# Attention and feed-forward fused on one core: both query blocks of a head pair transposed in one go, and ScalarE's queue in the order of the program

## The chip, the cores and the metric

The kernel runs on one core of one Trainium2 chip. The metric is the device time of one execution in microseconds, as the median over the runs; lower is better. The kernel before takes 610.69 us (median of 3 runs, 610.4 to 610.88).

## What is computed

Attention over 4 batches, 8 heads, 768 positions and head size 64, in which a query sees the 8 first positions and the 96 last ones up to itself, with a distance bias per head; its output, 3072 tokens of 512 features, goes through a gated feed-forward without an activation function.

```python
scores = scale * np.matmul(q, k.transpose(0, 1, 3, 2)) + bias
scores = np.where(keep, scores, -1000000000.0)
a = np.exp(scores - np.max(scores, axis=-1, keepdims=True))
a = a / (np.sum(a, axis=-1, keepdims=True) + 1e-09)
x = np.matmul(a, v)            # then heads side by side: 3072 x 512
out = (((x @ w1) * (x @ w2)) @ w3) @ w_out
```

All matmuls are float32 in precision: operands are split into a high and a low half in the matmul's own format, and three products are summed (high-high, low-high, high-low). The product w3 @ w_out is formed once, at the start.

## The kernel before, in words

**Chunks and visits.** A chunk is 256 tokens of one batch; there are 12. A head pair of a chunk is 128 rows of queries in two blocks of 128 (j = 0, 1). Two head pairs make a visit, so a chunk takes two visits and the loop has 24 of them (s = 0 to 23), and a last one (s = 24) with the values alone. A visit s does this:

- TensorE multiplies the transposed probabilities of visit s - 1 with the values (`values`, L457 and L459) into one PSUM bank, pool `ps_v`, tag "v"; then the scores of visit s (L406).
- ScalarE and VectorE split that result into a high and a low half, `xh` and `xl` (`split`, L63 and L64).
- VectorE takes the scores with the bias and their minimum (L421), ScalarE the exponentials and their sum (L422): eight of each, one for each head of each block.
- The scalings by 1/sum (`softmax`, L434): for each block the first head on ScalarE, the second on VectorE (L436). In the first four visits all eight are on ScalarE.
- Four turns (`flip`): two or four 128x128 transposes on TensorE (L445, L447) into one PSUM bank (`ps_t`, tag "t", one buffer), which ScalarE evicts to `ph` (L449). There is one for each head pair and query block. At the start of a sequence the first block has only half the keys, and two transposes.

**Feed-forward between them.** `FeedForward.run` is a generator over 512 tokens (two chunks; 256 for the first two runs). For each of 8 blocks f of the hidden width it multiplies with w1 (12 matmuls, tile `m`, n = 0), lets ScalarE evict that to `a` (L168), multiplies with w2 (n = 1), lets VectorE form the product `g` (L171) and ScalarE and VectorE split it (`gh`, `gl`). Then the output rows follow in four tiles of 24 matmuls (L178 to L180) that ScalarE evicts to `ot` (L184). All these results share two PSUM banks (pool `ps_m`, two buffers): the matmuls of the next f and n = 0 wait until `a` has been evicted, those of n = 1 until `g` has been formed. The generator yields at half and whole of each group of 12 matmuls; such a piece of six matmuls is a slice, and `slices(k)` puts the next k of them into the program. A run of 512 tokens has 48 slices, 12 a visit; the table `SLICES` says how many stand ahead of each turn and behind the last.

**What sets the order.** Each engine works through its queue in order. TensorE's order is that of the program text throughout (`manual_schedule`). In `first_steps` (visits 0 to 3, together with the loading and conversion of the weights and with w3 @ w_out, `fold`, L142) VectorE's and the DMA queue's are too. Elsewhere a scheduler orders the instructions by its own estimate; this holds for ScalarE everywhere. In the first steps VectorE also turns the weights' bits into the matmul format (L54, L56, L58), ScalarE takes their high halves (`w1h`, `w2h`, L122) and VectorE the low ones (L130); `fold_and_turn` puts the eight folds of one block between the turns.

## Time and profile before

| what | value |
|---|---|
| median of 3 runs | 610.69 us |
| the profiled execution | 609.55 us, of which the span of the instructions is 607.8 us |
| TensorE (PE) busy | 578.6 us, 95% of the span |
| ScalarE (ACT) busy | 287.6 us, 47% |
| VectorE (DVE) busy | 261.3 us, 43% |
| mean DMA rate | 89 GB/s |
| granted TensorE clock | 0.998 |

How to read it: PE is TensorE, PEld its weight loads, ACT ScalarE, DVE VectorE, SP the DMA queue's engine. In a row of the timeline stand the start in us from the start of the span, the duration, the engine, the line, the instruction, its tiles (out<-in), its shapes and how many were merged; in brackets the idle time of its engine just before it and who ended that. Matmuls overlap: each shows a duration that is longer than the step from one start to the next, so what TensorE loses is read from the starts.

### The profile page before, as it was taken

Reading aid. Unit: us, or ns where it says so; the run is one execution under the profiler, and the core shown is the slowest. Engines: PE = TensorE matmul, PEld = TensorE weight load, DVE = VectorE, ACT = ScalarE, POOL = GpSimd, SP = SyncE. Lnnn points to the kernel's source line nnn. Section 1 sums busy time; section 2 is a strip of 40 time slices with the busy share of each in tenths; the row PEclk is TensorE's granted clock in tenths of the full one; section 3 lists DMA queues with packets and bytes.
Section 4 is the critical chain, followed back from the end, with each engine's and each line's share of the span. In section 5 each row is a group of like instructions: output and inputs, shape, how many; then the busy total and the mean of one; then the engine's idle time right before and its main releaser. Section 6 shows DMA issues by size and latency. Waiting matters only on the chain.

```text
span 607.8 us, 9908 instructions
## 1 busy us (share of the span) xinstructions
PE 578.6 (95%) x3872; PEld 455.5 (75%) x3872; DVE 261.3 (43%) x851; ACT 287.6 (47%) x777; POOL 1.3 (0%) x10
## 2 busy tenths in 40 slices
PE   2998998999999999999999999999999999999995
PEld 0444568989977787887787887787878778888884
DVE  8999998432334424304442322542342451212200
ACT  3065677654455635525544544653553653522210
POOL 0000000000000000000000000000000000000000
PEclk9999999999999999999999999999999999999999
DMA  8897653222023202211220330120331120000001
GB/s 305 304 340 253 212 208 116 79 80 78 27 71 95 78 2 77 79 65 50 78 70 8 113 113 1 61 63 1 125 100 34 44 78 18 36 17 1 0 27 48
DMA packets 23240, 54.01 MB, mean 89 GB/s; under 512 B 2704, under 2 KB 4752, under 8 KB 23184
## 3 DMA queue, kind: packets, MB, share of 16 engines
q1 hardware_dynamic: 23184, 53.29, 25.7%
q8 instruction: 32, 0.52, 0.4%
q14 instruction: 24, 0.20, 0.1%
HBM read 46.99 MB, written 6.29 MB: 88 GB/s over the span
## 4 chain that ended last, share of the span: by engine, by line
PE 70%; ACT 13%; DVE 12%; issue 2%; DMA 2%; SPq 0%; DVEq 0%; ACTq 0%
PE m L161 11%; PE m L163 11%; PE m L162 10%; PE o L178 7%; PE o L180 7%; PE o L179 7%; ACT pr L422 7%; PE v L457 3%; PE t L445 3%; PE t L447 3%; ACT pr L434 3%; PE v L459 3%; PE w L142 2%; PE s L406 2%; DVE t L56 1%
## 5 line engine op out<-in xcount | busy, mean ns | idle before, releaser
L422 ACT ACTIVATE pr<-pr,mx 128x232 f32<-128x232 f32 (+1 forms) x192 | 88.4, 462 | 47.7 <-DVE mx L421 47.7
L449 ACT ACTIVATE ph<-t 128x512 f32<-128x512 f32 (+1 forms) x96 | 53.9, 561 | 101.5 <-PE t L447 93.1
L171 DVE TENSOR_TENSOR g<-m,a 128x512 f32<-128x512 f32 x48 | 33.2, 691 | 142.7 <-PE m L163 131.1
L161 PE MATMUL m<-xh,w1h 128*128 128x512 f32 (+1 forms) x224 | 85.8, 383 | 6.8 <-ACT a L168 6.8
L161 PE MATMUL m<-xh,w2h 128*128 128x512 f32 (+1 forms) x224 | 82.9, 370 | 0.3 <-ACT a L168 0.3
L163 PE MATMUL m<-xh,w1l 128*128 128x512 f32 (+1 forms) x224 | 80.8, 361 | 0.0
L162 PE MATMUL m<-xl,w1h 128*128 128x512 f32 (+1 forms) x224 | 80.7, 360 | 0.0
L163 PE MATMUL m<-xh,w2l 128*128 128x512 f32 (+1 forms) x224 | 80.7, 360 | 0.0
L162 PE MATMUL m<-xl,w2h 128*128 128x512 f32 (+1 forms) x224 | 80.5, 359 | 0.0
L178 PE MATMUL o<-wh,gh 128*128 128x512 f32 x192 | 78.2, 407 | 0.0
L180 PE MATMUL o<-wh,gl 128*128 128x512 f32 x192 | 75.3, 392 | 0.0
L179 PE MATMUL o<-wl,gh 128*128 128x512 f32 x192 | 75.0, 390 | 0.0
L142 PE MATMUL w<-wo,t 128*128 128x512 f32 x128 | 61.0, 622 | 12.1 <-DVE wo L58 11.2
L64 DVE TENSOR_TENSOR xl<-v,xh 128x512 fp32r<-128x512 f32 x24 | 16.6, 690 | 121.0 <-ACT xh L63 120.9
L63 ACT ACTIVATE gh<-g 128x512 fp32r<-128x512 f32 x48 | 30.2, 630 | 64.6 <-DVE g L171 64.6
L161 PEld LDWEIGHTS m<-xh,w1h 128*128 128x128 f32 x224 | 42.2, 189 | 20.0 <-ACT a L168 11.9
L142 PEld LDWEIGHTS w<-wo,t 128*128 128x128 f32 x128 | 24.1, 198 | 40.0 <-issue 22.4
L421 DVE CUSTOM_DVE_ANT_0 pr<-s,biasw 128x232 f32<-128x232 f32 x160 | 53.4, 394 | 0.0
L445 PE MATMUL t<-ident,pr 128*128 128x128 f32 x192 | 45.8, 273 | 3.7 <-ACT pr L434 3.4
L64 DVE TENSOR_TENSOR gl<-g,gh 128x512 fp32r<-128x512 f32 x48 | 33.2, 692 | 34.4 <-ACT gh L63 34.4
L161 PEld LDWEIGHTS m<-xh,w2h 128*128 128x128 f32 x224 | 42.3, 189 | 6.8 <-issue 0.7
L163 PEld LDWEIGHTS m<-xh,w1l 128*128 128x128 f32 x224 | 42.2, 189 | 6.7
(84 smaller groups left out, 816.1 us busy)
## 6 DMA issues: line engine op xcount, KB each, us to landing
qr<-qk SPq DMA_DIRECT2D x32, 312.0 KB, 3.8
vr<-vx SPq DMA_DIRECT2D x32, 256.0 KB, 3.0
stage<-w3t SPq DMA_DIRECT2D x15, 512.0 KB, 6.4
out_dram<-ot SPq DMA_DIRECT2D x24, 256.0 KB, 2.0
raws<-w SPq DMA_DIRECT2D x10, 512.0 KB, 5.7
qr<-qk SPq DMA_DIRECT2D x16, 260.0 KB, 3.4
vr<-vx SPq DMA_DIRECT2D x16, 192.0 KB, 2.7
stage<-w SPq DMA_DIRECT2D x6, 512.0 KB, 7.2
```

What stands on the lines that cost most here:

```text
L64: nc.vector.tensor_tensor(out=lo, in0=x, in1=hi.bitcast(F32), op=ALU.subtract)
L142: nc.tensor.matmul(ps, lhsT=self.t3[f, z][:, i * P:(i + 1) * P].bitcast(F32), rhs=self.wo[:, k].bitcast(F32), start=k == 0, stop=k == NFC - 1)
L161: nc.tensor.matmul(ps[:, z], lhsT=mh, rhs=xh[:, i], start=i == 0, stop=False)
L162: nc.tensor.matmul(ps[:, z], lhsT=mh, rhs=xl[:, i], start=False, stop=False)
L163: nc.tensor.matmul(ps[:, z], lhsT=ml, rhs=xh[:, i], start=False, stop=i == NCC - 1)
L178: nc.tensor.matmul(ps, lhsT=gh[:, f, ts], rhs=self.wh[:, f], start=f == 0, stop=False)
L179: nc.tensor.matmul(ps, lhsT=gh[:, f, ts], rhs=self.wl[:, f], start=False, stop=False)
L180: nc.tensor.matmul(ps, lhsT=gl[:, f, ts], rhs=self.wh[:, f], start=False, stop=f == NFC - 1)
L421: nc.vector.tensor_tensor_reduce(out=pr[:, j, u, w0:], in0=ps[u][:, j, w0:UW], in1=bias, scale=-SCALE, scalar=3.0e38, op0=ALU.add, op1=ALU ...
L422: nc.scalar.activation(pr[:, j, u, w0:], pr[:, j, u, w0:], AF.Exp, bias=m, scale=-1.0, accum_out=sm[:, j, u:u + 1])
L445: nc.tensor.transpose(pt[:, u, 0], pr[:, j, u, BW:UW], ident)
L449: nc.scalar.activation(ph[:, :, :nk], pt[:, :, :nk], AF.Copy)
```

## The change

The second query block of a head pair is transposed right behind the first, in the PSUM bank of the values, and `turn` does both. In the table each visit has two turns in place of four. In the loop from visit 4 on, ScalarE's order too is that of the program, and there the first two slices stand ahead of the scalings instead of behind them. In `fold_and_turn` the folds are divided 4, 3 and 1 around the two turns.

```diff
-        pt = ps_t.tile([P, 2, 2, P], F32, tag="t", name=f"t_{c}_{hp}_{j}")
+        pool, tag = ((ps_t, "t"), (ps_v, "v"))[j]
+        pt = pool.tile([P, 2, 2, P], F32, tag=tag, name=f"t_{c}_{hp}_{j}")
...
-    def turn(s, m, prs):
-        phs.setdefault(s, []).append(flip(*pairs(s)[m // NQ], m % NQ, prs[m // NQ][0]))
+    def turn(s, i, prs):
+        phs.setdefault(s, []).extend(flip(*pairs(s)[i], j, prs[i][0]) for j in range(NQ))
...
-            for m in range(STEP * NQ):
-                ff.fold(f, 2 * m, 2 * m + 1)
-                turn(s, m, prs)
+            ff.fold(f, 0, 1, 2, 3)
+            turn(s, 0, prs)
+            ff.fold(f, 4, 5, 6)
+            turn(s, 1, prs)
+            ff.fold(f, 7)
...
-        for m in range(STEP * NQ):
-            turn(3, m, prs)
-            slices(SLICES[3][m + 1])
+        for i in range(STEP):
+            turn(3, i, prs)
+            slices(SLICES[3][i + 1])
...
-    SLICES = [()] * 3 + [(4, 2, 2, 1, 1)] * 3 + [(4, 2, 1, 1, 1)] * 2 + [(5, 2, 2, 2, 1)] * (n - 8)
+    SLICES = [()] * 3 + [(4, 4, 2)] * 3 + [(4, 3, 2)] * 2 + [(5, 4, 3)] * (n - 8)
...
-        for s in range(4, n + 1):
-            rs = all_rows(s, visit(s))
-            for p, r in zip(pairs(s), rs):
-                softmax(*p, *r, nc.vector)
-            if s == n:
-                break
-            loads(s + 1)
-            for m in range(STEP * NQ):
-                slices(SLICES[s][m])
-                turn(s, m, rs)
-            slices(SLICES[s][-1])
-        slices(10 ** 6)
+        with tc.manual_schedule(engines={mybir.EngineType.Activation}):
+            for s in range(4, n + 1):
+                rs = all_rows(s, visit(s))
+                if s == n:
+                    break
+                slices(2)
+                for p, r in zip(pairs(s), rs):
+                    softmax(*p, *r, nc.vector)
+                loads(s + 1)
+                slices(SLICES[s][0] - 2)
+                for i in range(STEP):
+                    turn(s, i, rs)
+                    slices(SLICES[s][i + 1])
+            slices(10 ** 6)
```

Two places show what moves. The first is ScalarE's queue in a visit of the loop (visit 17, chunk 8; the lines of `flip` are two further down in the changed file). Before, from the exponentials (L422) on:

```order
L422 ACTIVATE pr_2_3641,sm_2_3643<-pr_2_3641,mx_2_3642 128x232 x4
L422 ACTIVATE pr_3_3652,sm_3_3654<-pr_3_3652,mx_3_3653 128x232 x4
L434 ACTIVATE pr_2_3641<-pr_2_3641,sm_2_3643 128x232 x2
L434 ACTIVATE pr_3_3652<-pr_3_3652,sm_3_3654 128x232 x2
L168 ACTIVATE a_3_3696<-m_3_0_3683 128x512
L63 ACTIVATE gh_3478<-g_3_3711 128x512
L449 ACTIVATE ph_2_0_3727<-t_2_0_3722 128x512
L168 ACTIVATE a_4_3735<-m_4_0_3715 128x512
L449 ACTIVATE ph_2_1_3749<-t_2_1_3744 128x512
L63 ACTIVATE gh_3478<-g_4_3757 128x512
```

and in the changed kernel:

```order
L422 ACTIVATE pr_2_3643,sm_2_3645<-pr_2_3643,mx_2_3644 128x232 x4
L422 ACTIVATE pr_3_3654,sm_3_3656<-pr_3_3654,mx_3_3655 128x232 x4
L168 ACTIVATE a_3_3678<-m_3_0_3665 128x512
L434 ACTIVATE pr_2_3643<-pr_2_3643,sm_2_3645 128x232 x2
L434 ACTIVATE pr_3_3654<-pr_3_3654,sm_3_3656 128x232 x2
L63 ACTIVATE gh_3460<-g_3_3713 128x512
L451 ACTIVATE ph_2_0_3729<-t_2_0_3724 128x512
L451 ACTIVATE ph_2_1_3736<-t_2_1_3731 128x512
L168 ACTIVATE a_4_3744<-m_4_0_3717 128x512
L63 ACTIVATE gh_3460<-g_4_3759 128x512
L451 ACTIVATE ph_3_0_3775<-t_3_0_3770 128x512
L451 ACTIVATE ph_3_1_3782<-t_3_1_3777 128x512
```

The eviction of the first feed-forward tile, `a_3`, has moved from behind the four scalings to ahead of them, and the evictions of a head pair's two blocks stand side by side. VectorE's and the DMA queue's orders are the same as before but for two swaps of neighbours on VectorE in visit 7.

The second place is TensorE's queue in the first steps, in `fold_and_turn(5, 1)` (`w_518` is the tile of the fold, `t_2` and `t_3` the two head pairs). Before:

```order
L142 MATMUL w_518<-wo,t_5_0_343 128x512 x2
L445 MATMUL t_2_0_521<-ident,pr_2_442 128x128 x2
L142 MATMUL w_518<-wo,t_5_0_343 128x512 x2
L445 MATMUL t_2_1_528<-ident,pr_2_442 128x128
L447 MATMUL t_2_1_528<-ident,pr_2_442 128x128
L445 MATMUL t_2_1_528<-ident,pr_2_442 128x128
L447 MATMUL t_2_1_528<-ident,pr_2_442 128x128
L142 MATMUL w_518<-wo,t_5_1_344 128x512 x2
L445 MATMUL t_3_0_537<-ident,pr_3_453 128x128 x2
L142 MATMUL w_518<-wo,t_5_1_344 128x512 x2
```

and in the changed kernel:

```order
L142 MATMUL w_518<-wo,t_5_0_343 128x512 x4
L447 MATMUL t_2_0_523<-ident,pr_2_442 128x128 x2
L447 MATMUL t_2_1_528<-ident,pr_2_442 128x128
L449 MATMUL t_2_1_528<-ident,pr_2_442 128x128
L447 MATMUL t_2_1_528<-ident,pr_2_442 128x128
L449 MATMUL t_2_1_528<-ident,pr_2_442 128x128
L142 MATMUL w_518<-wo,t_5_1_344 128x512 x3
L447 MATMUL t_3_0_538<-ident,pr_3_453 128x128 x2
```

Four folds stand ahead of the first turn instead of two, the second block follows the first without folds between, and one fold is left behind the last turn. ScalarE's queue, which the scheduler still orders here, has at this place:

```order
L451 ACTIVATE ph_2_0_526<-t_2_0_523 128x2x128
L451 ACTIVATE ph_2_1_533<-t_2_1_528 128x512
L451 ACTIVATE ph_3_0_541<-t_3_0_538 128x2x128
L451 ACTIVATE ph_3_1_548<-t_3_1_543 128x512
L144 ACTIVATE wh<-w_518 128x512
L122 ACTIVATE w1h<-t3s 128x512
L63 ACTIVATE xh_409<-v_2_565 128x2x256
L122 ACTIVATE w2h<-t3s 128x512
```

Before, `w1h` and `wh` stood between `ph_3_0` and `ph_3_1`, and `w2h` ahead of `xh`.

## The prediction

> **What bounds the kernel now.** I read the page first, then the list of waits, then the timeline of one visit of the loop and of the first steps. From the page come the span, TensorE's share and the clock:

> ```profile
> span 607.8 us, 9908 instructions
> ...
> PE 578.6 (95%) x3872; PEld 455.5 (75%) x3872; DVE 261.3 (43%) x851; ACT 287.6 (47%) x777; POOL 1.3 (0%) x10
> ...
> PEclk9999999999999999999999999999999999999999
> ```

> TensorE is busy for 95% of the span and the clock is full in all forty slices. An edit is worth what it takes from TensorE's waits, or adds. The list of waits (time in all, times, longest) names those that a turn or a scaling has part in:

> ```profile
> PE m L161 <- ACT a L168: 7.1, 13, 0.7
> ...
> PE t L445 <- ACT pr L434: 3.4, 2, 2.0
> ...
> DVE w2l L130 <- ACT w2h L122: 1.4, 3, 0.8
> ...
> DVE wl L147 <- ACT wh L144: 0.6, 1, 0.6
> ```

> The first is the largest: thirteen times the feed-forward's matmuls wait for a PSUM bank that `a` holds. The next rows are one such wait, from the timeline of visit 16, engine by engine (start, duration, engine, line, what; in brackets the idle time before and who ended it). TensorE, at the end of n = 1:

> ```profile
> 321.06 0.39 PE L162 MATMUL m<-xl,w2h 128*128 128x512 f32 x1
> 321.29 0.39 PE L163 MATMUL m<-xh,w2l 128*128 128x512 f32 x1
> 322.37 0.50 PE L161 MATMUL m<-xh,w1h 128*128 128x512 f32 x1 [0.69 <-ACT a L168]
> 322.71 0.39 PE L162 MATMUL m<-xl,w1h 128*128 128x512 f32 x1
> ```

> ScalarE and VectorE in the same stretch:

> ```profile
> 320.22 1.62 ACT L434 ACTIVATE pr<-pr,sm 128x232 f32<-128x232 f32 x4
> 321.74 0.57 ACT L168 ACTIVATE a<-m 128x512 f32<-128x512 f32 x1
> 323.07 0.63 ACT L63 ACTIVATE gh<-g 128x512 fp32r<-128x512 f32 x1 [0.76 <-DVE g L171]
> 324.51 0.60 ACT L449 ACTIVATE ph<-t 128x512 f32<-128x512 f32 x1 [0.80 <-PE t L447]
> ```

> ```profile
> 320.76 0.59 DVE L436 TENSOR_SCALAR pr<-pr,sm 128x232 f32<-128x232 f32 x2
> 322.35 0.69 DVE L171 TENSOR_TENSOR g<-m,a 128x512 f32<-128x512 f32 x1 [1.00 <-ACT a L168]
> ```

> The twelve matmuls of n = 1 take a step of 0.23 us each, so those of n = 0, which `a` evicts, were done about 12 steps before 321.29 + 0.39, at 318.9. ScalarE's exponentials end where its scalings begin, at 320.2; `a` stands behind the four scalings and starts only at 321.74. TensorE has then finished n = 1, and starts the next f at 322.37 instead of a step after 321.29.

> **The change part by part: `a` ahead of the scalings.** A matmul's step is 0.23 us (321.06 to 321.29). The wait makes it 1.08 us (321.29 to 322.37), 0.85 too long, and the next step is 0.34 instead of 0.23 (322.37 to 322.71), because the weight load starts late too: 0.96 us lost where the row reads 0.69 idle, so 0.27 more than the idle time each. Over the list: 7.1 us idle + 13 x 0.27 = 10.6 us. One of the thirteen lies in the first steps and is not of this kind:

> ```profile
> 100.79 0.39 PE L161 MATMUL m<-xh,w2h 128*128 128x256 f32 x1 [0.25 <-ACT a L168]
> ```

> It counts for 0.25 + 0.27 = 0.5 us; twelve waits in the loop remain, **10.1 us**. They are the three visits of each of four long runs that begin at n = 0 of some f.

> In the new order `a` stands right behind the exponentials. Its matmuls are done at 318.9, so it would start at 320.2 and end at 320.8; TensorE wants the bank at 321.5, a step after 321.29. The margin is 0.7 us and the whole wait goes. Where is the next one? `g` starts when the second group is done (321.29 + 0.39 = 321.7; VectorE's scalings end at 320.76 + 0.59 = 321.35) and ends at 322.4; its bank is wanted after twelve more matmuls and a turn of eight, at 321.5 + 2.7 + 0.9 = 325.1: margin 2.7 us. The scalings come 0.57 us later, 320.8 to 322.4, and a head pair needs half of them, by 321.6; the first turn stands behind one more slice, at 321.5 + 6 x 0.23 = 322.9: margin 1.3 us.

> **Two turns of eight for four of four.** The timeline of the same visit at its first turn:

> ```profile
> 323.87 0.27 PE L445 MATMUL t<-ident,pr 128*128 128x128 f32 x1
> 323.98 0.27 PE L447 MATMUL t<-ident,pr 128*128 128x128 f32 x1
> 324.09 0.27 PE L445 MATMUL t<-ident,pr 128*128 128x128 f32 x1
> 324.20 0.27 PE L447 MATMUL t<-ident,pr 128*128 128x128 f32 x1
> 324.23 0.48 PE L161 MATMUL m<-xh,w1h 128*128 128x512 f32 x1
> 324.55 0.39 PE L162 MATMUL m<-xl,w1h 128*128 128x512 f32 x1
> ```

> Four transposes with the matmul behind them take 323.87 to 324.55, 0.68 us, of which 0.23 is the matmul's: 0.45, or 0.11 each. There is no cost of going in and out, so eight in one go cost twice four: zero. Nor does ScalarE's count change.

> [...]

> **The bank of the values.** The second block needs that bank free. In each visit its last reader is VectorE's split, in this one:

> ```profile
> 315.38 0.69 DVE L64 TENSOR_TENSOR xl<-v,xh 128x512 fp32r<-128x512 f32 x1
> ```

> It ends at 316.1, 7 us ahead of the first turn. Between the turns lie four slices (24 x 0.23 = 5.5 us), behind the last three (4.1 us), and the two evictions take some 0.3 + 2 x 0.60 = 1.5 us after the last transpose (324.20 to 324.51, then the row's duration). The values queue behind this wait on TensorE, and everything behind them, but the margin is 2.6 us: zero.

> **The first steps.** TensorE's rows at visits 1 to 3, and ScalarE's scalings of visit 3:

> ```profile
> 59.56 0.62 PE L445 MATMUL t<-ident,pr 128*128 128x128 f32 x2 [2.05 <-ACT pr L434]
> ...
> 66.90 0.71 PE L457 MATMUL v<-ph,vr 128*64 128x128 f32 x8
> ...
> 96.41 0.33 PE L445 MATMUL t<-ident,pr 128*128 128x128 f32 x1 [1.38 <-ACT pr L434]
> ```

> ```profile
> 95.89 3.13 ACT L434 ACTIVATE pr<-pr,sm 128x232 f32<-128x232 f32 x8
> ```

> At 59.56 the first turn waits for the scalings; two more folds ahead of it fill most of that. A fold is 1.0 us at most: 7.34 us from 59.56 to 66.90, less twelve transposes at 0.11, by six folds. The values, at 66.90 now, would start up to 2 us earlier. But this is lent: at 96.41 the turn of visit 3 waits for scalings again, and those hang on VectorE's conversions, which run almost without a pause. So TensorE keeps only what VectorE gains: at most its waits for ScalarE in the list, 1.4 + 0.6 = 2.0 us, where a `ph` or scalings stood ahead of `w2h` or `wh`. I take half, 1.0. The new turn there needs two scalings more, at 3.13/8 = 0.39 us each, before it is through, and the four further transposes fill half of these 0.8 us, so it costs about 0.4; the wait of 0.5 at 100.79 goes, since `a` and `g` have that much more time. Together **1.0 us gained**, with bounds of nothing and 2.0.

> **Visits 4 to 7** have short runs whose first two slices end with `gh`, or with no eviction; it too goes ahead of scalings. In visit 4:

> ```profile
> 115.19 0.85 ACT L434 ACTIVATE pr<-pr,sm 128x232 f32<-128x232 f32 x2
> 115.95 0.62 ACT L63 ACTIVATE gh<-g 128x512 fp32r<-128x512 f32 x1
> 116.47 0.85 ACT L434 ACTIVATE pr<-pr,sm 128x232 f32<-128x232 f32 x2
> ```

> ```profile
> 116.72 0.27 PE L445 MATMUL t<-ident,pr 128*128 128x128 f32 x1
> ```

> With 0.52 us for `gh` (115.95 to 116.47) the first pair's scalings end at 116.56, and the turn starts at 116.72. That is close, but covered: zero; uncovered it could cost up to 0.5 us in each of three visits.

> **The sum.** 10.1 + 1.0 = 11.1 us off the profiled execution's 609.55 us (span 607.8 and 1.75 around it) gives 598.45. The median of the runs lies 1.14 us above that execution, so I forecast 599.6.

> **The rivals.**

> *The turn becomes the wait (6%).* A turn needs both blocks scaled, after an eviction that came in ahead. For it speaks that turns have waited for scalings twice (3.4 us above); against it the 1.3 us margin. If ScalarE were 1.6 us later than I reckon, the twelve visits would give back 0.3 us each: 603.2.

> *The first steps lose (6%).* With one fold (1.0 us) behind the last turn against 1.5 us of evictions, the values' bank holds TensorE 0.5 us in three visits, and VectorE gains nothing: 10.1 - 1.5, so 602.1.

> *The wait moves to `g` (4%).* `a` no longer blocks the first bank, but if VectorE formed `g` some 3.6 us later than I work out, n = 1 of the next f would wait in the twelve visits for as long as n = 0 did: about 609.7. Against it: VectorE's order is unchanged, and it idled a full 1.00 us for `a` at 322.35.

> *The hand-written queue blocks the values (3%).* Now ScalarE cannot pass over an instruction that is not ready. Were the second turn's evictions to sit behind a `gh` whose `g` waits for the last slices, TensorE would stand, at each of twelve visits, for `g`, `gh` and two evictions, 0.69 + 0.62 + 2 x 0.60 = 2.5 us: 30 us more against 11.1 less, 629.6. This decides as soon as the evictions come 2.6 us late. The order speaks against it: the last `gh` stands behind them.

> *The clock drops (1%).* [...] The clock row holds full through all groups of four and the 2.05 us pause. [...]

> **How the numbers follow.** The forecast has 80%. Its own range is the first steps' bounds, 598.6 to 600.6. The stated range goes down to 597.2, in case all of the 3.4 us that turns wait for scalings goes and not just 1.0, and up to 603.4 for the first two rivals. About 0.2%, 1.2 us, is what a measurement here can tell from no change. Faster: 80 + 6 + 6 = 92%; same: the 4% of the third rival; slower: 4%.

> **What would show it.** In the list of waits the row for `a` goes from thirteen to at most one. `a` starts within 0.1 us of the last exponential and TensorE's step over the boundary between two f is 0.23 us. If `t <-ACT pr` shows more than two waits, the first rival holds; a row `v <-ACT ph` means the bank of the values; `m <-DVE g` means the third. The values of visit 4, at 107.6 now, should start about 1 us earlier. A time over 603.4 or under 597.2 would make the prediction wrong.

## The result, and the profile after

The changed kernel takes 596.32 us (median of 4 runs, 595.49 to 597.13) where the kernel before takes 610.55: a ratio of 0.977 (95% interval 0.975 to 0.979), 14.2 us less. The forecast was 599.6 with a range down to 597.2, so the direction was right and the gain was underestimated, by more than the range allowed. The profiled execution took 596.74 us with a span of 595.0, 12.8 less than the 607.8 of before.

The page of the changed kernel, the lines that were shown of before:

```profile
span 595.0 us, 9954 instructions
...
PE 573.7 (96%) x3872; PEld 459.2 (77%) x3872; DVE 260.9 (44%) x851; ACT 284.4 (48%) x777; POOL 1.3 (0%) x10
...
PEclk9999998999999999999999999999999999999999
```

TensorE is still the bound. What is new is one slice below full clock, around 90 to 104 us; it comes up below. The list of waits (time in all, times, longest):

```profile
PE t L447 <- ACT pr L434: 2.4, 2, 2.1
...
PE t L447 <- DVE wl L147: 0.7, 1, 0.7
...
DVE w2l L130 <- ACT w2h L122: 0.3, 1, 0.3
```

The row of the feed-forward waiting for `a`, 7.1 us in thirteen waits, is gone altogether. Two turns wait for scalings, as before; VectorE's waits for `w2h` went from 1.4 to 0.3, those for `wh` went. One wait is new: a turn waits for `wl`.

The timeline of the place in the program that the prediction read (start, duration, engine, line, what). It lies in visit 14, and so did the prediction's rows, which call it visit 16: before, the values of visit 14 start at 313.12 us and those of visit 15 at 335.38. ScalarE:

```profile
313.95 0.47 ACT L422 ACTIVATE pr<-pr,mx 128x232 f32<-128x232 f32 x1
...
314.42 0.58 ACT L168 ACTIVATE a<-m 128x512 f32<-128x512 f32 x1
314.90 1.62 ACT L434 ACTIVATE pr<-pr,sm 128x232 f32<-128x232 f32 x4
316.67 0.63 ACT L63 ACTIVATE gh<-g 128x512 fp32r<-128x512 f32 x1 [0.15 <-DVE g L171]
317.67 1.09 ACT L451 ACTIVATE ph<-t 128x512 f32<-128x512 f32 x2 [0.37 <-PE t L449]
```

and TensorE:

```profile
315.45 0.39 PE L163 MATMUL m<-xh,w2l 128*128 128x512 f32 x1
315.68 0.39 PE L161 MATMUL m<-xh,w1h 128*128 128x512 f32 x1
...
316.81 0.39 PE L163 MATMUL m<-xh,w1l 128*128 128x512 f32 x1
317.04 0.27 PE L447 MATMUL t<-ident,pr 128*128 128x128 f32 x1
...
317.80 0.27 PE L449 MATMUL t<-ident,pr 128*128 128x128 f32 x1
317.83 0.48 PE L161 MATMUL m<-xh,w1h 128*128 128x512 f32 x1
318.14 0.40 PE L162 MATMUL m<-xl,w1h 128*128 128x512 f32 x1
```

`a` starts right behind the last exponential, and the step into the next f is 315.68 - 315.45 = 0.23 us where it was 1.08. The turn follows its predecessor without a pause, and its eight transposes take 317.04 to 318.14 less one step, 0.87 us, where the forecast's 0.11 for each gives 0.88.

Where did 12.8 us come from? The start of a visit's values cuts the program into stretches. Here are the rows for visits 4, 8 and 24, of before:

```profile
107.59 0.45 PE L457 MATMUL v<-ph,vr 128*64 128x128 f32 x4
...
181.00 0.44 PE L457 MATMUL v<-ph,vr 128*64 128x128 f32 x4
...
534.09 0.45 PE L457 MATMUL v<-ph,vr 128*64 128x128 f32 x4
```

and of the changed kernel:

```profile
106.67 0.34 PE L459 MATMUL v<-ph,vr 128*64 128x128 f32 x2
...
179.53 0.44 PE L459 MATMUL v<-ph,vr 128*64 128x128 f32 x4
...
521.12 0.45 PE L459 MATMUL v<-ph,vr 128*64 128x128 f32 x4
```

From visit 8 to 24, the sixteen visits with long runs, 353.09 us became 341.59: **11.50 us**. Up to visit 4 the values come 0.92 us earlier (106.67 for 107.59). Visits 4 to 7 give the rest of the 1.47 us at visit 8, **0.55 us**, nearly all in visit 7. The end of the program gives back 0.17. The forecast's terms for the same three stretches were 10.1, 1.0 and zero. These figures are not equally firm. The stretch from visit 8 to 24 takes 341.59 us in seven traces of this study, to the hundredth; but in five traces whose first steps are those of the changed kernel, the values of visit 4 start anywhere from 105.44 to 108.07 us, so 0.92 belongs to this one execution.

So the long visits gave 1.4 us more than forecast, and visits 4 to 7 half a microsecond that was not forecast. Which part of the change made them, the two traces alone do not tell.

### The profile page after: what moved, and what is told of

Read it like the earlier page. It is cut to its first block, busy times and chain, and to the rows that moved or that the text cites. A ratio compares the mean times of both kernels' runs of the same rounds, so it can differ in the third digit from the quotient of the medians.

```text
span 595.0 us, 9954 instructions
## 1 busy us (share of the span) xinstructions
PE 573.7 (96%) x3872; PEld 459.2 (77%) x3872; DVE 260.9 (44%) x851; ACT 284.4 (48%) x777; POOL 1.3 (0%) x10
## 5 line engine op out<-in xcount | busy, mean ns | idle before, releaser
L422 ACT ACTIVATE pr<-pr,mx 128x232 f32<-128x232 f32 (+1 forms) x192 | 88.4, 462 | 48.7 <-DVE mx L421 48.7
L171 DVE TENSOR_TENSOR g<-m,a 128x512 f32<-128x512 f32 x48 | 33.2, 691 | 133.2 <-PE m L163 132.5
L161 PE MATMUL m<-xh,w1h 128*128 128x512 f32 (+1 forms) x224 | 84.6, 378 | 0.0
L163 PE MATMUL m<-xh,w1l 128*128 128x512 f32 (+1 forms) x224 | 81.0, 361 | 0.0
L162 PE MATMUL m<-xl,w1h 128*128 128x512 f32 (+1 forms) x224 | 80.9, 361 | 0.0
L161 PE MATMUL m<-xh,w2h 128*128 128x512 f32 (+1 forms) x224 | 80.8, 361 | 0.0
L162 PE MATMUL m<-xl,w2h 128*128 128x512 f32 (+1 forms) x224 | 80.4, 359 | 0.0
L163 PE MATMUL m<-xh,w2l 128*128 128x512 f32 (+1 forms) x224 | 80.4, 359 | 0.0
L178 PE MATMUL o<-wh,gh 128*128 128x512 f32 x192 | 76.6, 399 | 0.0
L63 ACT ACTIVATE gh<-g 128x512 fp32r<-128x512 f32 x48 | 30.3, 630 | 94.2 <-DVE g L171 93.6
L142 PE MATMUL w<-wo,t 128*128 128x512 f32 x128 | 59.6, 615 | 11.7 <-DVE wo L58 11.2
L64 DVE TENSOR_TENSOR xl<-v,xh 128x512 fp32r<-128x512 f32 x24 | 16.6, 690 | 120.4 <-ACT xh L63 120.3
L451 ACT ACTIVATE ph<-t 128x512 f32<-128x512 f32 (+1 forms) x96 | 50.1, 558 | 30.1 <-PE t L449 18.9
L161 PEld LDWEIGHTS m<-xh,w1h 128*128 128x128 f32 x224 | 42.7, 191 | 8.5 <-issue 3.3
L64 DVE TENSOR_TENSOR gl<-g,gh 128x512 fp32r<-128x512 f32 x48 | 33.2, 692 | 33.2 <-ACT gh L63 33.2
L161 PEld LDWEIGHTS m<-xh,w2h 128*128 128x128 f32 x224 | 42.3, 189 | 7.0 <-issue 0.7
L163 PEld LDWEIGHTS m<-xh,w1l 128*128 128x128 f32 x224 | 42.6, 190 | 6.5
L162 PEld LDWEIGHTS m<-xl,w2h 128*128 128x128 f32 x224 | 42.3, 189 | 6.4
```

Of the source, the lines that this page charges most:

```text
L64: nc.vector.tensor_tensor(out=lo, in0=x, in1=hi.bitcast(F32), op=ALU.subtract)
L142: nc.tensor.matmul(ps, lhsT=self.t3[f, z][:, i * P:(i + 1) * P].bitcast(F32), rhs=self.wo[:, k].bitcast(F32), start=k == 0, stop=k == NFC - 1)
L161: nc.tensor.matmul(ps[:, z], lhsT=mh, rhs=xh[:, i], start=i == 0, stop=False)
L162: nc.tensor.matmul(ps[:, z], lhsT=mh, rhs=xl[:, i], start=False, stop=False)
L163: nc.tensor.matmul(ps[:, z], lhsT=ml, rhs=xh[:, i], start=False, stop=i == NCC - 1)
L171: nc.vector.tensor_tensor(out=g, in0=ps, in1=a, op=ALU.mult)
```

## The experiments

There were eleven runs, two of them repeats, in three groups, each group on one chip beside its own runs of before (medians 610.49, 609.96 and 609.85 us).

**One part alone.** `a` alone is the kernel before with ScalarE's order and the early slices, and four separate turns as they were:

```diff
-        for s in range(4, n + 1):
-            rs = all_rows(s, visit(s))
-            for p, r in zip(pairs(s), rs):
-                softmax(*p, *r, nc.vector)
...
+        with tc.manual_schedule(engines={mybir.EngineType.Activation}):
+            for s in range(4, n + 1):
+                rs = all_rows(s, visit(s))
...
+                slices(2)
+                for p, r in zip(pairs(s), rs):
+                    softmax(*p, *r, nc.vector)
...
```

> The kernel before with ScalarE's feed-forward evictions ahead of the scalings in the loop, and nothing else: four separate turns in one bank, first steps as before. Main theory: `a` is worth 10.7 us (twelve waits, read from the starts of the values) and visits 4 to 7 some 0.6, so 11.3 us less than before, about 599.3. The forecast's own terms (10.1 and zero for visits 4 to 7) give 600.4. Rival: the whole gain comes from `a`, and merging the turns and the first steps are worth nothing: 14.2 less, about 596.4. The list of waits has no row of a loop's matmul waiting for `a` by any of them.

The turns alone is the changed kernel with the reverse of this edit:

> The changed kernel with the scalings ahead of the feed-forward's slices again in the loop, as before (ScalarE ordered by the scheduler there): merged turns, the second block in the bank of the values, first steps of the changed kernel. Main theory: a merged turn saves 0.08 us per visit, 1.3 us over the sixteen visits with long runs and a little in visits 4 to 7, and the first steps 1 to 2 us: 2.5 to 3.5 us less than before, 607 to 608. The forecast's own terms (merging zero, first steps 1.0): 609.5. Rival: without the early `a` the merged turns lose, because eight transposes ask for four scalings at once: slower than before. The waits for `a` stay at twelve or thirteen.

The third takes the changed kernel's loop with the first steps of before:

```diff
...
-            ff.fold(f, 0, 1, 2, 3)
-            turn(s, 0, prs)
-            ff.fold(f, 4, 5, 6)
-            turn(s, 1, prs)
-            ff.fold(f, 7)
+            for m in range(STEP * NQ):
+                ff.fold(f, 2 * m, 2 * m + 1)
+                turn_one(s, m, prs)
...
```

> The changed kernel with the first steps (up to visit 3) as before: one block at a time in the turns' own bank there, the loop as changed. Main theory: the loop is worth 12 to 13 us and the first steps 1 to 2: this kernel takes about 597.3, and TensorE's step between matmuls stays at full speed behind visit 3, where the changed kernel shows 0.21 us per transpose for some 3 us behind a wait of 2.1 us; its runs should lie close together, without the changed kernel's two groups of times 1.4 us apart. Rival: the first steps are worth nothing: the same time as the changed kernel. Rival: the slow stretch has nothing to do with the longer wait, and comes here as well.

And the changed kernel itself:

> The changed kernel once more, on the chip of the three others, for comparison. 595 to 597 us; if the slow stretch behind visit 3 comes in some executions only, the times fall into two groups about 1.4 us apart, near 595.6 and 597.

Medians of five or six runs: `a` alone 599.95 us (ratio 0.983, 0.9815 to 0.9844), the turns alone 607.38 (0.995, 0.9935 to 0.9964), the first steps of before 598.30 (0.9805, 0.9789 to 0.982), the changed kernel 596.82 (0.9777, 0.9762 to 0.9791). So `a` is worth 10.5 us and the turns 3.1, together 13.6, and the changed kernel shows 13.7: in the medians the parts add up. Stretch by stretch they do so less well, and the differences cancel: in the long visits the turns alone save 0.86 us (352.23 for 353.09), which with the 10.19 of `a` below makes 11.05 and not 11.50; in visit 7 each part alone saves nearly what both save together (0.54 and 0.56 us for 0.60). The first steps are worth 1.5 of the whole (598.30 to 596.82), merging the turns behind them, with its second bank, 1.65 (599.95 to 598.30). The rival by which all came from `a` falls, and so does the one by which merged turns lose without it.

The values of visits 8 and 24 with `a` alone:

```profile
181.44 0.43 PE L457 MATMUL v<-ph,vr 128*64 128x128 f32 x3
...
524.34 0.43 PE L457 MATMUL v<-ph,vr 128*64 128x128 f32 x3
```

342.90 us, 10.19 less than before: the twelve waits were worth what the forecast said, 10.1. My theory's 10.7 after the result had put part of the turns' gain down to them. The changed kernel saves 1.31 us more in this stretch. There `a` alone shows, behind a turn of four:

```profile
326.15 0.27 PE L447 MATMUL t<-ident,pr 128*128 128x128 f32 x1
326.18 0.48 PE L178 MATMUL o<-wh,gh 128*128 128x512 f32 x1
326.50 0.39 PE L179 MATMUL o<-wl,gh 128*128 128x512 f32 x1
326.73 0.40 PE L180 MATMUL o<-wh,gl 128*128 128x512 f32 x1
326.97 0.39 PE L178 MATMUL o<-wh,gh 128*128 128x512 f32 x1
327.19 0.40 PE L179 MATMUL o<-wl,gh 128*128 128x512 f32 x1
327.43 0.39 PE L180 MATMUL o<-wh,gl 128*128 128x512 f32 x1
327.66 0.39 PE L178 MATMUL o<-wh,gh 128*128 128x512 f32 x1
```

The first step behind the turn is 0.32 us, and the next ones 0.23, 0.24, 0.22, 0.24 and 0.23 before they settle; over the stretch the medians are 318, 231, 236, 228, 231 and 231 ns, and then 227. Going in and out of a turn therefore has a price that one timeline rounded to hundredths hides.

**Is it the entry, or the bank?** The merged turns differ from four separate ones in two ways: TensorE goes into transposes half as often, and the second block has a bank of its own. Two kernels tell these apart. In the first, a visit enters its transposes six times instead of twice:

```diff
...
+            if u == 0:
+                slices(mid)
...
+    def three_turns(s, i, prs):
+        phs.setdefault(s, []).append(flip(*pairs(s)[i], 0, prs[i][0], 1))
+        slices(1)
+        phs[s].append(flip(*pairs(s)[i], 1, prs[i][0]))
...
-                    turn(s, i, rs)
-                    slices(SLICES[s][i + 1])
+                    (turn if s < 8 else three_turns)(s, i, rs)
+                    slices(SLICES[s][i + 1] if s < 8 else (1, 2)[i])
```

> The changed kernel, but in visits 8 to 23 each pair's first block turned in two pieces (one per head) with a slice between, and a slice between the blocks: six entries of transposes per visit where the changed kernel has two, the same transposes, banks, evictions and number of slices. Theory: each entry costs TensorE about 0.04 us (the matmuls behind a turn take 318, 231, 235, 228 and 231 ns where undisturbed ones take 227, and the boundary of a turn is some ns longer), so 64 more entries cost 2.6 us: about 599.2 if the changed kernel takes 596.6 here. The forecast's term (no cost of going in and out): no difference. Rival: the gain beside `a` came from the evictions' place or from the bank, and this stays within 0.5 us of the changed kernel.

In the second, `a` alone gets the second bank and stays with four separate turns:

```diff
-        pt = ps_t.tile([P, 2, 2, P], F32, tag="t", name=f"t_{c}_{hp}_{j}")
+        pool, tag = ((ps_t, "t"), (ps_v, "v"))[j]
+        pt = pool.tile([P, 2, 2, P], F32, tag=tag, name=f"t_{c}_{hp}_{j}")
```

> The kernel with `a` alone moved ahead (four separate turns, first steps as before), and the second block's turn in the bank of the values instead of the turns' own. Theory of 0.04 us per entry: the long visits stay as they were with `a` alone; only the two waits of a turn for an eviction in visits 5 and 6, 0.3 us each, can go, so 599.3 to 599.9 where `a` alone took 599.95. Rival: the gain of the merged turns over `a` alone, 1.65 us, comes from two banks in alternation: about 598.3. Second rival: the bank of the values is claimed too late and the values wait: slower than 600.5, with a row of the values waiting for the eviction.

Six entries: 598.78 us (0.9808, 0.979 to 0.9825). The values of visits 8 and 24:

```profile
180.92 0.44 PE L461 MATMUL v<-ph,vr 128*64 128x128 f32 x4
...
524.49 0.34 PE L461 MATMUL v<-ph,vr 128*64 128x128 f32 x2
```

343.57 us, 1.98 more than the changed kernel for 64 more entries (2.5 by the medians, each against its own runs of before): 0.031 us each. No wait of TensorE is listed in these visits, so it is all in the steps. From four entries to two it was 1.31 us for 32: 0.041 each. The bank alone: 598.49 us (0.9811, 0.9794 to 0.9827), less than the 599.3 to 599.9 of the theory and near the rival's number, but its trace says otherwise:

```profile
180.06 0.33 PE L458 MATMUL v<-ph,vr 128*64 128x128 f32 x2
...
522.96 0.34 PE L458 MATMUL v<-ph,vr 128*64 128x128 f32 x2
```

342.90 us, the same as `a` alone to the hundredth. In the long visits the bank is worth nothing. What it gains lies earlier: at visit 8 it is 1.38 us ahead of `a` alone (180.06 and 181.44). It spares the two turns in visits 5 and 6 that with `a` alone start 0.3 us late, by the expectation for the eviction of the bank they share (a step of 0.42 us in place of 0.12; this is the one in visit 6):

```profile
160.72 0.28 PE L163 MATMUL m<-xh,w1l 128*128 128x256 f32 x1
161.14 0.44 PE L445 MATMUL t<-ident,pr 128*128 128x128 f32 x2
```

And it shortens the waits for scalings in the first steps, from 3.4 to 2.0 us. In the first steps it also shows what the forecast's second rival had feared, the values held up by evictions right behind the last turn (no fold stands between them there), from its list of waits:

```profile
PE v L458 <- ACT ph L450: 2.2, 3, 0.7
PE t L446 <- ACT pr L434: 2.0, 2, 1.1
```

The changed kernel leaves a fold or slices behind the last turn and has no such row; it was not run without them.

**The margin of the scalings.** Four slices ahead of the scalings instead of two put `gh` ahead too:

```diff
-                slices(2)
+                slices(2 if s < 8 else 4)
...
-                slices(SLICES[s][0] - 2)
+                slices(SLICES[s][0] - (2 if s < 8 else 4))
```

> The changed kernel with four slices' evictions ahead of the scalings in visits 8 to 23 instead of two, so that `gh` or the output's eviction, too, stands ahead of them. The forecast gave the turn a margin of 1.3 us against its scalings; `gh` can start only when `g` is formed, so the scalings come 2.5 us later: the turn waits 1.0 to 1.2 us in each of twelve visits, 609 to 611 where the changed kernel takes 596.6, with a row of the turn waiting for the scalings, twelve times and more. Rival: the margin is larger than worked out and the time hardly moves, under 599.

606.04 us (0.9938, 0.9924 to 0.9952), 3.8 less than its runs of before, where the changed kernel's are 13.7 less: 9.9 us lost, less than expected, but the mechanism and the count are the expected ones. Its list of waits, and TensorE at a turn:

```profile
PE t L447 <- ACT pr L434: 8.7, 13, 2.2
```

```profile
365.01 0.39 PE L163 MATMUL m<-xh,w1l 128*128 128x512 f32 x1
365.93 0.33 PE L447 MATMUL t<-ident,pr 128*128 128x128 f32 x1 [0.54 <-ACT pr L434]
```

The turn comes 0.92 - 0.23 = 0.69 us late. The scalings start 2.78 us behind `a` here (365.41 and 362.63) and 0.48 in the changed kernel (314.90 and 314.42), 2.30 later; so the margin is 2.30 - 0.69 = 1.6 us where 1.3 had been worked out, and `gh` uses it up. Two slices are the right number here.

**The first steps.** The longest wait left is that of visit 3's turn. It hangs on sums that stand behind a conversion of weights in VectorE's queue, so I put the first pair's sums and scalings ahead of it:

```diff
+        softmax(*pairs(3)[0], *prs[0], nc.scalar)
+        slices(2)
         w12(6)
-        slices(2)
-        scale(3)
+        softmax(*pairs(3)[1], *prs[1], nc.scalar)
+        loads(4)
```

> The changed kernel with the first pair's sums and scalings of visit 3 ahead of the sixth conversion of weights instead of behind it. Theory: the turn of visit 3 waits 2.1 us for scalings whose sums stand behind 3.1 us of conversions; with them ahead, it starts about 1.5 to 2.0 us earlier, and nothing later wants the conversion in time: 594.8 to 595.3 where the changed kernel takes 596.8. If the half clock behind that wait hangs on its length, it goes as well: mean clock 0.998 or more in every execution and about 593.8. Rival: the gain is taken back by the next wait (the feed-forward for its eviction or for the weights whose conversion is now later): same as the changed kernel. Rival on the clock: the half clock comes by chance, and the clocks stay mixed between 0.994 and 0.999.

and, the other way, all scalings of visit 3 (`scale(3)`) behind the seventh conversion (`w12(7)`):

> The changed kernel with all of visit 3's scalings behind the seventh conversion too, so that TensorE's wait in front of that turn grows from 2.1 us to 5 to 7. If the half clock comes from the wait's length, it comes in every execution: mean clock 0.996 or less each time, a slice of the clock row under full speed, and the time rises by the wait (3 to 5 us) and about 1.2 more against the fastest runs of the changed kernel: 598.5 to 602. If it comes by chance, the clocks stay mixed between 0.994 and 0.999.

The early scalings take 595.01 us (0.9747, 0.9731 to 0.9763), and once more, in the third group, 594.76 (0.9752, 0.974 to 0.9765):

> The version with visit 3's first scalings early once more, on the chip of the two others: 595.0, and mean clocks of 0.997 or more in every execution, if the half clock hangs on the length of the wait.

That is 1.3 to 1.4 us better than the changed kernel of the first group, measured each against its own runs of before (1.8 and 2.1 by the medians as they stand), and the fastest version of the study. The first expectation of a turn 1.5 to 2.0 us earlier holds: the step into it is 0.3 us too long in place of 2.3. But 1.2 of these 2.0 us go to two new waits for `a` behind it, 0.2 and 1.0, of which the list of the repeated run names the larger:

```profile
PE m L161 <- ACT a L168: 0.9, 1, 0.9
```

So 0.8 us of it stay, and to them comes that the clock no longer drops (mean clocks of 0.997 to 0.999 in all ten executions). The longer wait takes 601.68 us (0.9854, 0.9837 to 0.9871), 5.4 more than the changed kernel by the same reckoning:

```profile
PE t L447 <- ACT pr L434: 6.9, 2, 6.6
```

Its mean clocks are 0.993 and 0.994. The section on the hardware comes back to this.

The last one undoes the new wait of the first turn for `wl`, on top of the early scalings (the last argument of `flip`, False, keeps the second block in the turns' own bank):

```diff
...
+            if s == 0:
+                for m in range(STEP * NQ):
+                    ff.fold(f, 2 * m, 2 * m + 1)
+                    phs.setdefault(s, []).append(flip(*pairs(s)[m // NQ], m % NQ, prs[m // NQ][0], False))
+                return
```

> The version with visit 3's first scalings early, and the turn of visit 0 as before the change: one block at a time in the turns' own bank, folds between. In the changed kernel that turn's second block waits 0.9 to 1.3 us for VectorE, since the bank of the values still holds a fold's product there (wl is its last reader). The forecast's step (TensorE keeps only what VectorE gains): the wait goes, the values of visit 1 start about 1 us earlier, but those of visit 2 do not, since TensorE then waits for the scalings of visit 1 instead; the time is that of the version it is made from, about 595.0. Rival: TensorE keeps what that wait costs: about 594.0.

595.75 us (0.9766, 0.9753 to 0.978): no faster, if anything slower. Its values of visits 1 and 2:

```profile
44.65 0.33 PE L459 MATMUL v<-ph,vr 128*64 128x128 f32 x2
...
64.76 0.33 PE L459 MATMUL v<-ph,vr 128*64 128x128 f32 x2
```

and those of the version that it is made from, in the same group:

```profile
45.52 0.44 PE L459 MATMUL v<-ph,vr 128*64 128x128 f32 x4
...
64.35 0.33 PE L459 MATMUL v<-ph,vr 128*64 128x128 f32 x2
```

At visit 1 it is 0.87 us ahead, at visit 2 it is 0.41 behind: TensorE's time saved there is lent, as the prediction put it: it is not kept. Since the same first steps do not take the same time in every execution (the values of visit 2 start at 64.71 us in the trace of the changed kernel, at 64.35 in that of the early scalings), the distance between the two visits says it better: 20.11 us here, and 18.83 and 18.84 in the two traces of the early scalings.

## Why the prediction was right and wrong

**`a` ahead of the scalings: right.** 10.1 us forecast, 10.19 in the trace and 10.5 by the medians of `a` alone. The late weight load, which the prediction charged beside the idle time, is in the trace of before: behind the wait it starts at 322.37 us, 1.11 us after the end of the one ahead of it, where those ahead start 0.23 us apart (320.61, 320.84, 321.07). The margin of 1.3 us for the turns was right in kind, and 1.6 in size: with two slices ahead no turn of the loop waits, with four the first turn of each of the twelve visits does.

**Two turns of eight for four of four: this step failed.** "There is no cost of going in and out, so eight in one go cost twice four: zero." The runs show 0.03 to 0.04 us for each entry: 1.31 us for the 32 that the change removes, 1.98 us for 64 that were added. I had counted the transposes and one matmul behind them; the disturbance runs on through five more matmuls at 1 to 9 ns each, and the step into a turn has a median of 230 ns in the long visits of the kernel before, 3 more than the 227 of an undisturbed one. Per entry that is about one part in six of a matmul's step; times 32 it is 1.3 us, as much as the 1.2 that the prediction took a measurement here to resolve.

**The bank of the values: right in the long visits** (no difference at all in 16 visits), but wrong as "in each visit its last reader is VectorE's split". In visit 0 the bank still holds a fold's product, whose last reader is `wl`; the first turn waits 0.7 us for it here and 1.1 us in the kernel with six entries. The first turn apart shows that this costs nothing in the end.

**Visits 4 to 7: zero was wrong by 0.55 us.** The danger I named, scalings late for the turn, did not come. In visit 7 `gh` goes ahead of the scalings and the output's matmuls no longer wait for it and for `gl`; this gain is there with `a` alone too (0.56 us), and with the turns alone, where the longer turn gives `gh` the time (0.54). What could have cost something was the shared bank: with `a` alone, visits 5 and 6 lose 0.36 us each, which the second bank prevents.

**The first steps: the size.** 1.0 us forecast with bounds of nothing and 2.0, 1.5 by the medians. That TensorE keeps only what VectorE gains stands, by the experiment on the first turn and by the turns alone: there visit 3's scalings start 2.17 us earlier than before (93.72 for 95.89) and the values of visit 4 come 2.15 earlier (105.44 for 107.59). "I take half" was too cautious, as VectorE's waits went nearly all, from 2.0 to 0.3 us. In the profiled execution of the changed kernel only 0.92 is seen, in part because the clock took some of it back.

**From the profiled execution to the median: this failed too, by 1.6 us.** "The median of the runs lies 1.14 us above that execution" was taken over to the changed kernel. Its own profiled execution lies 0.42 above its median, not 1.14 below. Executions differ with their mean clock: of the third group's runs of before, the four with a mean clock of 0.996 or less take 610.33 to 610.65 us, six of the other seven 609.26 to 609.85. The trace of before has no drop in the first steps, that of the changed kernel has one, so the place of the first among its runs could not be carried over to the second. Together: 1.31 + 0.55 and the small rest make the profiled run 1.7 us faster than the sum, and this step adds 1.6: 3.3 us, the distance from 599.6 to 596.3. Either miss alone would have left the time inside the stated range, which went down to 597.2 (599.6 less 1.7 is 597.9, less 1.6 it is 598.0); it took both.

**The rivals.** None came in the changed kernel. The wait for scalings and the values' bank are real: four slices ahead made the first bind, and the second did so in the first steps of the bank alone. The fifth rival, a drop of the clock, did not come in the loop: turns of eight step at 109 ns throughout, as turns of four do at 108. No run shows a drop that transposes bring. But in the first steps the clock did drop, behind a wait: in the trace of the changed kernel it is at half before the turn's first transpose starts (94.57 and 94.62 us). That the row of before was full through a pause of 2.05 us spoke less against it than the prediction took it to, as the last section shows.

## What to carry to other kernels

In a queue that is bound by one engine, an eviction that frees a PSUM bank goes ahead of work whose user comes later, as long as the margin of that user is not spent: one item ahead gained 10 us, a second one gave nearly all of it back. Changing between transposes and matmuls had a price here, 0.03 to 0.04 us for each entry, that shows only if one averages the steps for some ten instructions behind the change, in ns and not in hundredths of a us; times the number of changes it can decide. And before the place of one profiled execution among the runs is carried over, see whether its clock and theirs are alike; one traced drop, or none, says little about the next execution: with waits of 2.0 to 2.2 us the low mean clock came in 36 of 69.

## What the runs showed of the hardware

In the trace of the changed kernel TensorE's clock is at half behind a wait of 2.14 us. Its TensorE at visit 3:

```profile
94.62 0.47 PE L447 MATMUL t<-ident,pr 128*128 128x128 f32 x1 [2.14 <-ACT pr L434]
94.89 0.42 PE L449 MATMUL t<-ident,pr 128*128 128x128 f32 x1
...
96.60 0.41 PE L162 MATMUL m<-xl,w1h 128*128 128x256 f32 x1
96.81 0.41 PE L163 MATMUL m<-xh,w1l 128*128 128x256 f32 x1
```

Transposes and matmuls step by 0.21 us there. In the turns alone the wait in front of this turn is 2.14 us as well, but the clock stays full: the matmuls step by 0.12 us, the transposes, which hang on the scalings there, by 0.17 and 0.21 in turn. The windows of that stretch (from and to, length, then the busy time of PE, PEld, DVE, ACT and POOL, the granted clock, DMA), of the changed kernel:

```profile
91.15:94.57 3.42, 1.33 (x12) 1.13 (x10) 3.35 (x9) 3.14 (x11) 0.00 (x0) 1.00 0.76 305
94.57:97.98 3.41, 3.36 (x16) 3.22 (x17) 3.41 (x8) 3.41 (x9) 0.00 (x0) 0.50 0.00 0
97.98:101.39 3.41, 3.41 (x30) 3.41 (x30) 1.05 (x3) 2.36 (x5) 0.00 (x0) 1.00 0.02 5
```

and of the turns alone:

```profile
89.38:92.80 3.42, 2.73 (x23) 2.53 (x22) 3.42 (x12) 3.14 (x13) 0.00 (x0) 1.00 1.01 379
92.80:96.21 3.41, 1.96 (x13) 1.42 (x14) 3.34 (x11) 3.41 (x9) 0.00 (x0) 1.00 0.11 43
```

The half clock lasts 3.41 us here; behind the 6.6 us wait of the longer pause it is still 0.50 from 102 to 103 us, where the turn started at 99.01. From the start of visit 3's turn to the values of visit 4 it is 11.19 us in the turns alone, and 12.05, 12.50, 12.52 and 12.39 in the four traces with a drop behind a wait of this length (the changed kernel, its repeat, the six entries, four slices ahead), so a drop cost 0.9 to 1.3 us. Sorted by TensorE's longest wait in the trace of the same kernel (behind the first 11 us wait for weights), executions with a mean clock of 0.996 or less (that is what the traces with a drop in the first steps have; those without have 0.997 or more) were: none of 20 where it is 1.1 us or shorter (the bank alone, the early scalings, the first turn apart), 36 of 69 where it is 2.0 to 2.2 (before and all others), 5 of 5 at 6.6 us. So in these runs it goes with the length of the wait, and at 2.0 to 2.2 us it came in some executions and not in others. Two expectations failed on this: the first steps of before, with a wait of 2.0 us, were to keep the clock, and two of five executions lost it; the repeat of the changed kernel was to show two groups of times, and all five of its executions lost it.
